# The first columns of w_in in f32 on SyncE's queue, and batch 1's kv products by halves

## Chip, cores, metric

The kernel runs on one core of a Trainium2 chip. The metric is the device time of one execution in microseconds (us). Engine names are those of the profile: PE is TensorE (PEld its weight loads), ACT ScalarE, DVE VectorE, POOL GpSimd, SP SyncE.

## What is computed

Two blocks follow each other: a linear attention and a feed-forward layer with a "snake" activation. Cut to what matters:

```python
# q, k, v: (8 batches, 8 heads, 576 tokens, 64)
q_s = softmax(q, axis=-1)          # over the 64 features of a token
k_s = softmax(k, axis=2)           # over the 576 tokens
kv  = einsum('bhsd,bhse->bhde', k_s, v)
att = einsum('bhsd,bhde->bhse', q_s, kv)

x = att.transpose(0, 2, 1, 3).reshape(4608, 512)    # tokens x model dim
h = x @ w_in                       # (512, 2048)
g = h + sin(alpha * h)**2 / alpha
out = g @ w_out                    # (2048, 512)
```

All inputs and the output are f32 in HBM; the kernel multiplies in bf16.

## The kernel before

**Tiling.** A batch has 576 tokens, held as 64 groups of J = 9 tokens (P = 64); with two head groups (e) that makes 128 partitions. `xT`, the transposed input of the feed-forward layer, lies in SBUF as 4 blocks of 128 model dims by 4608 tokens. The feed-forward layer goes over the tokens in nine tiles of MF = 512, which don't fall together with the batches: token tile 0 needs batch 0's first 8 of 9 groups, tile 1 needs the ninth and 7 of batch 1's, and so on. d_ff is cut in nN = 16 blocks of 128.

**Attention of a batch.** ScalarE takes exponentials of q and k (`exp_q`, `exp_k`, L117). `norm_q` (L139 to L146) sums and divides on VectorE, or on VectorE and GpSimd; TensorE (L186) or a DMA (L196) transposes the result into `qT`. v is cast into `vb` with a column of ones (`cast_v`, L131). `kv_mm` (L157) multiplies keys by values: for a model-dim half ii, 9 x 2 products of 64 rows by 130 columns. `kv_norm` (L167, L170) divides by the column of sums into `kbd`, a block-diagonal matrix, whose halves of the model dims are [:, e, ii]. `attn_out` (L206, evicted at L209) or `attn_chunk` (L214) multiplies `qT` by `kbd` into PSUM, which a copy casts into `xT`.

**Feed-forward of a token tile.** `mm_h` (L234) does four products of 512 columns for each of 16 blocks; `sine` takes the sine on ScalarE (L240) and the square on ScalarE (L242), GpSimd (L244) or VectorE (L246); `combine` on VectorE (L250) makes g. `mm_o` (L254) does 64 products of 512 columns for a tile, evicted at L260 and stored at L263. `take(os, n)` puts the next n of these output products into TensorE's order, so they can be laid between other work. The order of each engine's work is that of the program text (`manual_schedule`); each engine takes its instructions in order.

**The start.** SyncE's queue carries q, k and v of batch 0 (L94, L275). GpSimd waits for the first half of k (`held`, L313) and then issues the loads of w_in, which cast f32 to bf16 on their way (L107): columns 0 to 255, 256 to 511, and three times 512 columns, each as two DMAs, one for each half x of the model dims; then the first two of four parts of w_out (L110). The view of w_in is

```python
win_v = moe_w_in.rearrange("(x c d) n -> x d c n", x=2, c=4)
```

so the row of w_in is x * 256 + c * 64 + d: partition 64 x + d holds it in block c. TensorE does warm-up products (L302), batch 0's transposes, kv and output products, and begins token tile 0 with the products of blocks 0 and 1 (columns 0 to 255 of w_in). Loads of batch 1's q and k are issued within token tile 0, after blocks 6 and 13 (`late`). The loads use a pool of 5 staging tiles (`stage`), taken in turn.

**Batch 1** lies in token tile 0's output products: 10 of them, the ninth group of batch 0 (L214, copied at L390), 36 more, the transposes, 12 more, both halves of kv, one norm over both, 3 more, and then for each half two `attn_out` of 4 and 5 groups and one output product. Two PSUM buffers (`ps_e`) serve the kv and output products. Then token tile 1 begins. Its output products (`o_stream(1)`) carry batch 2's attention in the same way.

Of the kernel before, what the change touches and what calls it, by code (L numbers as in the profile page):

```python
# [15 lines left out]
F32 = mybir.dt.float32  # L16
# [7 lines left out]
def kernel(  # L24
# [14 lines left out]
    nc = tc.nc  # L39
    ctx.enter_context(nc.allow_non_contiguous_dma(reason="layout"))  # L40
    B, H, S, D = q.shape
# [3 lines left out]
    J = 9  # L45
    P = S // J
# [8 lines left out]
    stage = ctx.enter_context(tc.tile_pool(name="stage", bufs=5))  # L55
# [11 lines left out]
    xT = singles.tile([128, 4, NT], BF16, name="xT")  # L67
    win = singles.tile([128, 4, d_ff], BF16, name="win")
# [7 lines left out]
    def src_view(t, b):  # L76
        return t[b].rearrange("(i e) (p j) d -> (e p) i (j d)", e=2, j=J)

    win_v = moe_w_in.rearrange("(x c d) n -> x d c n", x=2, c=4)
# [5 lines left out]
    def load(name, t, b, halves=False, eng=nc.sync, gate=None):  # L85

        st = stage.tile([128, 4, J, D], F32, name=f"st_{name}", tag="st")
        for ii in range(2) if gate else ():
            gate(st[:, ii, 0, 0:1], zero)
        view = src_view(t, b)  # L90
        flat = st.rearrange("p i j d -> p i (j d)")
        if halves:
            for ii in range(2):
                eng.dma_start(out=flat[:, ii::2], in_=view[:, ii::2])  # L94
        else:
            eng.dma_start(out=flat, in_=view)
        staged[name, b] = st
# [6 lines left out]
    def load_win(c0, c1):  # L104
        n = slice(c0, c1)
        for x in range(2):
            nc.gpsimd.dma_start(out=win[64 * x:64 * x + 64, :, n], in_=win_v[x][:, :, n])  # L107

    def load_wout(c):
        nc.gpsimd.dma_start(out=wout[:, 4 * c:4 * c + 4, :], in_=wout_v[:, 4 * c:4 * c + 4, :])  # L110
# [38 lines left out]
    def kv_mm(b, ii, pool, split=False):  # L149

        if ii == 0 or split:
            A["kvp", b] = pool.tile([128, 2, 512], F32, name="kvp", tag="a")
        kvp, ke, vt = A["kvp", b], A["ke", b], vb[b % 2]
        for j in range(J):
            for e in range(2):
                r = slice(64 * e, 64 * e + 64)
                nc.tensor.matmul(kvp[:, e, ii * 130:(ii + 1) * 130],  # L157
                                 ke[r, j, ii * 128:(ii + 1) * 128],
                                 vt[r, j, ii * 130:(ii + 1) * 130],
                                 start=(j == 0), stop=(j == J - 1))  # L160

    def kv_norm(b, i0=0, i1=2):

        kt, m = kbd[b % 2], i1 - i0
        kvr = small.tile([128, 2, 2, 2], F32, name="kvr")[:, :, 0:m]
        src = A["kvp", b][:, :, i0 * 130:i1 * 130].rearrange("p e (ii x c) -> p e ii x c", ii=m, x=2)
        nc.vector.reciprocal(kvr, src[:, :, :, :, D])  # L167
        for x in range(2):
            r = slice(64 * x, 64 * x + 64)
            nc.vector.tensor_tensor(kt[r, :, i0:i1, r], src[r, :, :, x, 0:D],  # L170
                                    kvr[r, :, :, x].unsqueeze(3).to_broadcast([64, 2, m, D]), op=ALU.mult)
# [28 lines left out]
    def attn_out(b, ii, half, pool, eng):  # L200
        qT, kt = A["qT", b], kbd[b % 2]
        j0, j1 = XO[half]
        n = (j1 - j0) * P
        xp = pool.tile([128, 2, 512], F32, name="xp", tag="a")
        for e in range(2):
            nc.tensor.matmul(xp[:, e, 0:n], kt[:, e, ii], qT[:, ii, j0:j1, e * 64:(e + 1) * 64],  # L206
                             start=True, stop=True)
        c0 = (J * b + j0) * P
        eng(xT[:, 2 * ii:2 * ii + 2, c0:c0 + n], xp[:, :, 0:n])  # L209

    def attn_chunk(b, c, j0, j1, xp):

        ii, e = divmod(c, 2)
        nc.tensor.matmul(xp, kbd[b % 2][:, e, ii], A["qT", b][:, ii, j0:j1, e * 64:(e + 1) * 64],  # L214
                         start=True, stop=True)
# [6 lines left out]
    def mm_h(t, ni, wide=None, k0=0, k1=4):  # L222

        if ni == 0 and k0 == 0:
            G[t] = gpool.tile([128, nN, MF], BF16, name="g")
        if k0:
            hp = HP[t, ni]
        elif wide and ni % 6 in ((2, 3) if t == 0 else (4, 5)):
            hp = wide()
        else:  # L230
            hp = ps_h.tile([128, MF], F32, name="hp", tag="h")
        HP[t, ni] = hp
        for ki in range(k0, k1):
            nc.tensor.matmul(hp, win[:, ki, ni * 128:(ni + 1) * 128],  # L234
                             xT[:, ki, t * MF:(t + 1) * MF], start=(ki == 0), stop=(ki == 3))
        return hp
# [30 lines left out]
    ACT_CP, DVE_CP, GP_CP = nc.scalar.copy, nc.vector.tensor_copy, nc.gpsimd.tensor_copy  # L267
# [6 lines left out]
    for ii, j0, j1 in VJ:  # L274
        nc.sync.dma_start(out=st[:, ii::2, j0:j1].rearrange("p i j d -> p i (j d)"),  # L275
                          in_=src_view(v, 0)[:, ii::2, j0 * D:j1 * D])
    make_identity(nc, ident)
    DVE_CP(identb, ident)
    zero = singles.tile([128, 1], F32, name="zero")
# [7 lines left out]
    ps_e = ES.enter_context(tc.tile_pool(name="ps_e", bufs=2, space=PSUM, reuse_waits="tile"))  # L287
# [23 lines left out]
    q_tile(0)  # L311

    GP_CP(singles.tile([128, 1], F32, name="held"), staged["k", 0][:, 0, 0, 0:1])  # L313
    for c0, c1 in ((0, 256), (256, 512), (512, 1024), (1024, 1536), (1536, 2048)):
        load_win(c0, c1)
    for c in range(2):
        load_wout(c)
    q_transpose_ii(0, 0, 0, 8, tps[0])
# [14 lines left out]
    for c in range(4):  # L333
        xp = ps_h.tile([128, MF], F32, name="hp", tag="h")
# [4 lines left out]
    def h_slot(t, ni, sq, lag, wide=None):  # L339
        hp = mm_h(t, ni, wide, 2 if t < 2 and ni < 2 else 0)  # L340
        lag.append((t, ni, hp, sine(t, ni, hp, sq)))

    def flush(lag, keep):
        while len(lag) > keep:
            combine(*lag.pop(0))
# [14 lines left out]
    def take(it, n=1000):  # L360
        for _ in range(n):
            if next(it, 0) == 0:
                return
# [4 lines left out]
    with ES:  # L368
        def lent():
            return ps_e.tile([128, 2, MF], F32, name="hh", tag="a")[:, 0]  # L370

        late = {6: lambda: load("q", q, 1, halves=True, gate=DVE_CP), 8: lambda: load_wout(2),
                10: lambda: load_wout(3), 13: lambda: load("k", k, 1, halves=True, gate=DVE_CP)}
        for ki in range(2):
            for ni in range(2):
                mm_h(0, ni, lent, ki, ki + 1)
        for ni in range(nN):
            h_slot(0, ni, "DPAPPAPPAPPAPPAP"[ni], lag, lent)
            flush(lag, 1)
            if ni in late:  # L380
                late[ni]()
        flush(lag, 0)

        accs = [ps_h.tile([128, dm], F32, name="hp", tag="h") for _ in range(4)]
        os = o_quad(0, accs, [DVE_CP, ACT_CP, DVE_CP, ACT_CP])
        take(os, 10)
        xp = ps_e.tile([128, 4, P], F32, name="xp", tag="a")
        for c in range(4):
            attn_chunk(0, c, 8, 9, xp[:, c])
        ACT_CP(xT[:, :, 8 * P:9 * P], xp)  # L390
        take(os, 36)
        exp_q(1)
        load("v", v, 1, halves=True)
        load_batch(2)
        norm_q(1, [GP, V])
        exp_k(1)
        for ii in range(2):
            q_transpose(1, ii, ps_e, DVE_CP)
        cast_v(1, [ACT_CP, DVE_CP])
        nc.scalar.activation(zero, zero, AX.Sin)  # L400
        take(os, 12)
        kv_mm(1, 0, ps_e)
        kv_mm(1, 1, ps_e)
        kv_norm(1)
        take(os, 3)
        for ii in range(2):
            attn_out(1, ii, 0, ps_e, DVE_CP)
            attn_out(1, ii, 1, ps_e, ACT_CP)
            take(os, 1)
        take(os)  # L410
        load("q", q, 3)
        load("k", k, 3)

        for ki in range(2):
            for ni in range(2):
                mm_h(1, ni, lent, ki, ki + 1)
        for ni in range(nN):
            h_slot(1, ni, SQ[ni], lag, lent)
            flush(lag, 1)
        cast_v(2, [GP_CP, GP_CP])  # L420
        flush(lag, 0)

    ps_o = ctx.enter_context(tc.tile_pool(name="ps_o", bufs=2, space=PSUM, reuse_waits="tile"))
    ps_a = ctx.enter_context(tc.tile_pool(name="ps_a", bufs=1, space=PSUM, reuse_waits="tile"))
# [12 lines left out]
    exp_q(2)  # L437
    exp_k(2)
    os = o_stream(1)
    take(os, 16)  # L440
    norm_q(2, [GP, V])
    exp_q(3)
    exp_k(3)
# [11 lines left out]
    c0 = J * 2 * P  # L455
    for c in range(4):
        xp = ps_h.tile([128, MF], F32, name="hp", tag="h")[:, 0:6 * P]
# [3 lines left out]
    xp = ps_a.tile([128, 2, 512], F32, name="xp", tag="a")[:, :, 0:6 * P]  # L461
# [27 lines left out]
    for t in range(3, nT):  # L489
        b = t + 1 if t + 1 < B else None  # L490
        os = o_stream(t - 1)
# [56 lines left out]
```

The softmax here doesn't subtract the row's maximum and nothing guards it: scores larger than these inputs give would overflow.

## Time and profile before

| | |
|---|---|
| time, median of 3 runs | 291.37 us (291.19 to 291.61) |
| span of the profiled execution | 289.5 us |
| TensorE's first product of token tile 0 (L234) | starts at 15.38 us |
| TensorE's first product of token tile 1 (L234) | starts at 49.24 us |
| w_in's loads (L107) | issued from 8.82 to 15.3 us, 3.9 to 10.0 us from issue to landing |
| TensorE, ScalarE, VectorE, GpSimd busy | 95%, 79%, 65%, 28% of the span |

The page of the profile gives the busy time of each engine in the span, then a row for each engine over 40 equal slices of 7.24 us, in which a digit is the busy share in tenths. Busy time of TensorE is a model: a product of 512 columns is shown with 379 ns, but in a stream the next one starts 216 ns later, so what a stream takes is read from starts. A line of the timeline gives the start, the time that a run of equal instructions takes, engine and line, the operation with the tiles it writes and reads, how many there are, and in brackets how long the engine was idle before and what ended that. A line of the list of waits gives who waited for whom: the total, how often, the longest. A line of the DMA view gives for each queue its packets, MB and the time of its packets as a share of 16 DMA engines' time (over 100% when packets overlap); q1 is SyncE's queue, q0 GpSimd's.

### The profile page before, as it was taken

To read this page: it belongs to the slowest core of one execution; us is meant where nothing else is said; L and a number is where in the kernel's file an instruction comes from. 1 tells how busy PE (TensorE), PEld (TensorE's weight loads), DVE (VectorE), ACT (ScalarE), POOL (GpSimd) and SP (SyncE) were. 2 spreads that over 40 slices of the span, in tenths; PEclk is the share of its full clock that TensorE was granted. 3 is DMA by queue.
4 is the path that set the end of the run, shared out by engine and by line. 5 is a ranking of instruction groups with operands and counts; after the bars stand their busy time and mean duration, and the time that the engine had idled before them with its cause. 6 is when DMAs were issued, how large, how long until landed. Compare 5 with 4: busy or idle time off the path is not lost.

```text
span 289.5 us, 4230 instructions
## 1 busy us (share of the span) xinstructions
PE 274.8 (95%) x1543; PEld 131.2 (45%) x1570; DVE 187.7 (65%) x277; ACT 227.6 (79%) x322; POOL 80.4 (28%) x74
## 2 busy tenths in 40 slices
PE   2989998999999999999999999999999999999995
PEld 1434454444454445444444454445444444444443
DVE  3967586798958658774777567756775555545412
ACT  4789755999569899889987998799987777777500
POOL 0968420676685635002600070005000000000000
PEclk9999999999999999999999999999999999999999
DMA  7999999944899965109901893113311111111142
GB/s 263 306 174 232 275 371 408 310 189 135 201 161 389 399 198 127 33 20 344 314 14 33 298 307 77 37 39 84 70 39 36 36 36 39 36 37 36 39 110 72
DMA packets 37893, 45.77 MB, mean 158 GB/s; under 512 B 15968, under 2 KB 21360, under 8 KB 37872
## 3 DMA queue, kind: packets, MB, share of 16 engines
q1 hardware_dynamic: 32848, 41.16, 46.0%
q0 software_dynamic: 4832, 4.20, 9.4%
q8 instruction: 12, 0.20, 0.3%
q10 hardware_dynamic: 192, 0.14, 0.2%
q14 instruction: 9, 0.07, 0.1%
HBM read 36.71 MB, written 9.44 MB: 159 GB/s over the span
## 4 chain that ended last, share of the span: by engine, by line
PE 82%; DVE 6%; ACT 3%; POOL 3%; DMA 3%; issue 2%; ACTq 0%
PE hp L234 35%; PE op L254 34%; PE hp L254 4%; PE kvp L157 3%; POOL s L244 2%; PE xp L206 2%; DVE qs L144 2%; ACT s L240 1%; DMA st_q<-in_q_dram 1%; DMA qT<-qn 1%; PE op L234 1%; DVE g L250 1%; PE op L518 1%; PE hh L234 1%; DVE qn L146 1%
## 5 line engine op out<-in xcount | busy, mean ns | idle before, releaser
L250 DVE SCALAR_TENSOR_TENSOR g<-s,inva_sb,hp 128x512 bf16<-128x512 f32 x130 | 95.6, 746 | 63.9 <-ACT s L242 52.1
L234 PE MATMUL hp<-xT,win 128*128 128x512 bf16 x513 | 129.2, 379 | 1.2 <-DMA win<-in_moe_w_in_dram 0.6
L254 PE MATMUL op<-wout,g 128*128 128x512 bf16 x478 | 121.5, 379 | 1.4 <-issue 0.6
L240 ACT ACTIVATE s<-hp,alpha_sb 128x512 f32<-128x512 f32 x130 | 87.7, 682 | 26.5 <-PE hp L234 25.7
L234 PEld LDWEIGHTS <-win 128*128 128x128 bf16 x576 | 56.2, 98 | 68.9 <-issue 2.7
L254 PEld LDWEIGHTS <-g 128*128 128x128 bf16 x560 | 54.1, 98 | 61.8 <-issue 0.6
L242 ACT ACTIVATE s<-s 128x512 f32<-128x512 f32 x112 | 70.5, 630 | 3.6
L146 POOL TENSOR_TENSOR qn<-qe,qs 128x1152 bf16<-128x1152 bf16 x12 | 25.3, 2129 | 80.1 <-DVE qs L140 68.0
L244 POOL TENSOR_TENSOR s<-s 128x512 f32<-128x512 f32 x29 | 30.5, 1064 | 26.7 <-ACT s L240 26.2
L260 DVE COPY o<-op 128x512 f32<-128x512 f32 (+2 forms) x33 | 21.8, 662 | 9.9 <-PE op L254 6.0
L117 ACT ACTIVATE ke<-st_k 128x1152 bf16<-128x1152 f32 x16 | 17.8, 1151 | 4.2 <-DMA st_k<-in_k_dram 2.3
L139 DVE TENSOR_REDUCE qs<-qe 128x36 f32<-128x2304 bf16 x5 | 12.8, 2553 | 11.0 <-ACT qe L117 10.9
L117 ACT ACTIVATE qe<-st_q 128x1152 bf16<-128x1152 f32 x16 | 17.8, 1155 | 2.4 <-DMA st_q<-in_q_dram 2.4
L131 POOL CAST vb<-st_v 128x1152 bf16<-128x1152 f32 x12 | 13.6, 1165 | 5.9 <-DMA st_v<-in_v_dram 5.9
L209 DVE CAST xT<-xp 128x512 bf16<-128x512 f32 (+1 forms) x20 | 14.7, 736 | 0.7 <-PE xp L206 0.6
L254 PE MATMUL hp<-wout,g 128*128 128x512 bf16 x62 | 14.6, 379 | 0.2 <-issue 0.2
L144 DVE TENSOR_REDUCE qs<-qe 128x18 f32<-128x1152 bf16 x6 | 8.0, 1330 | 4.6 <-ACT qe L117 4.6
L206 PE MATMUL xp<-qT,kbd 128*128 128x256 bf16 (+1 forms) x48 | 9.5, 286 | 1.4 <-ACT xT L209 0.9
L117 ACT ACT_TABLE_LOAD x7 | 9.0, 1283 | 1.3 <-PEq L532 1.2
L157 PE MATMUL kvp<-vb,ke 64*128 64x130 bf16 x288 | 9.7, 216 | 0.0
L157 PEld LDWEIGHTS <-ke 64*128 64x128 bf16 x288 | 8.2, 93 | 3.2 <-issue 2.3
L234 PE MATMUL hh<-xT,win 128*128 128x512 bf16 x40 | 9.4, 379 | 0.0
(64 smaller groups left out, 115.3 us busy)
## 6 DMA issues: line engine op xcount, KB each, us to landing
out_dram<-o SPq DMA_DIRECT2D x70, 128.0 KB, 2.3
st_q<-in_q_dram SPq DMA_DIRECT2D x6, 1152.0 KB, 6.6
st_k<-in_k_dram SPq DMA_DIRECT2D x6, 1152.0 KB, 8.5
st_v<-in_v_dram SPq DMA_DIRECT2D x6, 1152.0 KB, 10.3
st_q<-in_q_dram SPq DMA_DIRECT2D x4, 576.0 KB, 5.8
st_k<-in_k_dram SPq DMA_DIRECT2D x4, 576.0 KB, 7.3
wout<-in_moe_w_out_dram POOLq DMA_DIRECT2D x4, 512.0 KB, 12.6
st_v<-in_v_dram SPq DMA_DIRECT2D x3, 576.0 KB, 10.7
```

What stands on the lines that cost most here:

```text
L117: nc.scalar.activation(dst[:, :, ii * 128:(ii + 1) * 128].rearrange("p j (x d) -> p x j d", x=2), src[:, ii::2], AX.Exp)
L146: engs[ii % len(engs)].tensor_tensor(qn[:, ii].rearrange("p j (x d) -> p j x d", x=2), qe[:, ii], part.unsqueeze(3).to_broadcast([128, J, ...
L157: nc.tensor.matmul(kvp[:, e, ii * 130:(ii + 1) * 130], ke[r, j, ii * 128:(ii + 1) * 128], vt[r, j, ii * 130:(ii + 1) * 130], start=(j == 0 ...
L206: nc.tensor.matmul(xp[:, e, 0:n], kt[:, e, ii], qT[:, ii, j0:j1, e * 64:(e + 1) * 64], start=True, stop=True)
L209: eng(xT[:, 2 * ii:2 * ii + 2, c0:c0 + n], xp[:, :, 0:n])
L234: nc.tensor.matmul(hp, win[:, ki, ni * 128:(ni + 1) * 128], xT[:, ki, t * MF:(t + 1) * MF], start=(ki == 0), stop=(ki == 3))
L240: nc.scalar.activation(s, hp, AX.Sin, scale=alpha_sb[:, ni:ni + 1])
L242: nc.scalar.activation(s, s, AX.Square)
L244: nc.gpsimd.tensor_tensor(s, s, s, op=ALU.mult)
L250: nc.vector.scalar_tensor_tensor(G[t][:, ni], in0=s, scalar=inva_sb[:, ni:ni + 1], in1=hp, op0=ALU.mult, op1=ALU.add)
L254: nc.tensor.matmul(acc, G[t][:, ni, j * 128:(j + 1) * 128], wout[:, ni, :], start=(ni == 0), stop=(ni == nN - 1))
L260: eng(o[:, cols], acc)
```

## The change

It has two parts. In the first, the first 256 columns of w_in no longer come by a casting DMA of GpSimd's queue: four DMAs on SyncE's queue, behind v, bring them in f32 into a staging tile, and GpSimd casts them (`GP_CP`) after it has issued the loads of columns 256 to 1535, and before those of columns 1536 up. It is meant to have the first columns there early, and to take their transfer out of GpSimd's queue. In the second, batch 1's kv products, norm and output products go by model-dim half, each half in a PSUM tile of its own, with output products of token tile 0 between them, so that TensorE has work while VectorE norms a half. Only the 7 groups that token tile 1 needs are made there; the other 2 come within the output products of token tile 1, in one copy.

```diff
         nc.sync.dma_start(out=st[:, ii::2, j0:j1].rearrange("p i j d -> p i (j d)"),
                           in_=src_view(v, 0)[:, ii::2, j0 * D:j1 * D])
+
+    wf = stage.tile([128, 4, J, D], F32, name="st_w", tag="st")[:, :, 0:4].rearrange("p c a b -> p c (a b)")
+    for c in range(4):
+        nc.sync.dma_start(out=wf[:, c], in_=win_v[:, :, c, 0:256])
...
     GP_CP(singles.tile([128, 1], F32, name="held"), staged["k", 0][:, 0, 0, 0:1])
-    for c0, c1 in ((0, 256), (256, 512), (512, 1024), (1024, 1536), (1536, 2048)):
+    for c0, c1 in ((256, 512), (512, 1024), (1024, 1536)):
         load_win(c0, c1)
+    GP_CP(win[:, :, 0:256], wf)
+    load_win(1536, 2048)
     for c in range(2):
         load_wout(c)
...
-        take(os, 12)
-        kv_mm(1, 0, ps_e)
-        kv_mm(1, 1, ps_e)
-        kv_norm(1)
-        take(os, 3)
+        take(os, 8)
+        kv_mm(1, 0, ps_e, split=True)
+        kv_norm(1, 0, 1)
+        take(os, 2)
+        kv_mm(1, 1, ps_e, split=True)
+        kv_norm(1, 1, 2)
+        take(os, 1)
+
+        c0 = J * P
         for ii in range(2):
-            attn_out(1, ii, 0, ps_e, DVE_CP)
-            attn_out(1, ii, 1, ps_e, ACT_CP)
-            take(os, 1)
+            xp = ps_e.tile([128, 2, 512], F32, name="xp", tag="a")[:, :, 0:7 * P]
+            for e in range(2):
+                attn_chunk(1, 2 * ii + e, 0, 7, xp[:, e])
+            (ACT_CP, DVE_CP)[ii](xT[:, 2 * ii:2 * ii + 2, c0:c0 + 7 * P], xp)
+            take(os, 2)
         take(os)
...
     os = o_stream(1)
-    take(os, 16)
+    take(os, 8)
+    xp = ps_a.tile([128, 4, 2 * P], F32, name="xp", tag="a")
+    for c in range(4):
+        attn_chunk(1, c, 7, 9, xp[:, c])
+    DVE_CP(xT[:, :, (J + 7) * P:2 * J * P], xp)
+    take(os, 8)
     norm_q(2, [GP, V])
```

## The prediction

> **What bounds the kernel now.** I read the engine shares and the row by slices first, then TensorE's waits, then the timelines of the two stretches that the change touches, then the DMA queues there.
>
> ```profile
> PE 274.8 (95%) x1543; PEld 131.2 (45%) x1570; DVE 187.7 (65%) x277; ACT 227.6 (79%) x322; POOL 80.4 (28%) x74
> ...
> PE   2989998999999999999999999999999999999995
> ...
> DMA  7999999944899965109901893113311111111142
> ```
>
> TensorE is full from the third slice to the last, so a change pays only where TensorE idles, and any new idle time is added to the end one for one. The DMA row is full over the first seven slices (50 us): this is where the change puts its transfers. The waits of TensorE (total, times, longest) are few:
>
> ```profile
> PE xp L206 <- ACT xT L209: 0.9, 2, 0.6
> ...
> PE hp L214 <- DVE kbd L170: 0.6, 2, 0.4
> PE hp L234 <- DMA win<-in_moe_w_in_dram: 0.6, 1, 0.6
> PE xp L206 <- DVE kbd L170: 0.4, 1, 0.4
> ```
>
> The third is w_in's: the timeline of TensorE at the start has
>
> ```profile
> 15.38 1.95 PE L234 MATMUL hp<-xT,win 128*128 128x512 bf16 x7
> 17.17 1.89 PE L234 MATMUL hh<-xT,win 128*128 128x512 bf16 x8
> 19.61 0.59 PE L234 MATMUL hp<-xT,win 128*128 128x512 bf16 x2 [0.55 <-DMA win<-in_moe_w_in_dram]
> ```
>
> so columns 0 to 511 are there in time at 15.38, and 0.55 us is lost on columns 512 up. The L206 waits are batch 1's, in this stretch:
>
> ```profile
> 44.28 1.40 PE L157 MATMUL kvp<-vb,ke 64*128 64x130 bf16 x36
> 45.84 0.59 PE L254 MATMUL hp<-wout,g 128*128 128x512 bf16 x2 [0.16 <-issue]
> 46.88 0.66 PE L206 MATMUL xp<-qT,kbd 128*128 128x256 bf16 x4 [0.44 <-DVE kbd L170]
> ...
> 48.32 0.65 PE L206 MATMUL xp<-qT,kbd 128*128 128x256 bf16 x4 [0.57 <-ACT xT L209]
> ```
>
> Last, the DMA queues (packets, MB, share of 16 engines), first in 5 to 9 us, where SyncE's queue is alone, then in 27 to 41 us, where it meets GpSimd's:
>
> ```profile
> q1 hardware_dynamic: 759, 1.64, 104.2%
> ```
> ```profile
> q1 hardware_dynamic: 1361, 2.97, 58.1%
> q0 software_dynamic: 1305, 1.29, 54.8%
> ```
>
> Alone it moves 1.64 MB in 4 us, 410 GB/s, so 25.6 GB/s for each of 16 engines. GpSimd's queue alone, in 16 to 24 us, writes 1.60 MB in bf16, 200 GB/s. Where both have work, each has about half of the engines' time.
>
> **What the Trainium skill says.** "DMA: Bandwidth & Descriptors", section "Why a DMA increments its semaphore by 16 and not by 1": a DMA need not use all 16 engines. The generator takes the slowest dimension (of a size other than 1) of source and of destination and uses the largest number up to 16 that divides both; for SyncE these are the lowest-numbered engines. Every load in the kernel before has 128, 64 or 16 there, so its trace shows only the case of 16 and can't confirm the rule. The same page, "Queues, rings and completion order": each engine goes round the queues that have work for it, packet by packet, and within one queue in order; the half shares of 27 to 41 us agree. "TensorE: Matmul & The Clock Gate", section "The HAM clock gate": after an idle window of some 3.4 us TensorE runs at half rate until it has been busy about as long. The trace agrees at its start: warm-up matmuls (L302) follow each other at 0.43 us from 5.81 to 10.15, and 512-column matmuls at 0.216 later (16 in 3.62 us with an end of 0.38).
>
> **The new w_in load.** The four DMAs read win_v[:, :, c, 0:256]: 2 halves (x) of 64 rows of 256 columns; x and d don't merge, since c lies between them. Source 2, destination 128: the rule gives **2 engines**, the same two for all four DMAs. The present loads avoid this, as each takes one x and has 64 on both sides.
>
> Landing. The DMAs stand behind v in SyncE's queue; v is read out at 11.7 (q1 moves its last 0.14 MB within 11 to 12). They carry 4 x 128 x 1 KB = 0.524 MB, 0.262 MB on each of two engines: at 25.6 GB/s, 10.2 us. From 11 us these engines also have their sixteenth of GpSimd's loads: columns 256 to 1535 are 1.31 MB in bf16, at 200 GB/s 6.5 us. Both queues must be served, and at half shares GpSimd's part is done first, so w lands at 11.7 + 10.2 + 6.5 = 28.4. If SyncE's queue were always served first: 11.7 + 10.2 = 21.9.
>
> The cast. GpSimd casts 128x1152 in 1.17 us (L131), so 128x1024 in 1.04; with 0.3 for hand-over, columns 0 to 255 are ready at 29.8. The first product of the first token tile needs them, and TensorE takes its work in order: it starts at 29.8 where it started at 15.38. **Cost 14.4 us**, nothing beside it, for TensorE has nothing else to do. Behind the cast, GpSimd holds the load of columns 1536 up (needed ten products' pace later, some 10 us; 0.26 MB halves land in about 4 us on a free queue), the first two w_out loads (needed after 14 us) and the squares of L244 (issue ends 2.9 us after the cast, first square needed at about 3.2): I cost these at nothing, hidden by ScalarE's 13.7 us of sines and squares in that tile.
>
> After 14 us idle TensorE is cold: some 9 of its first matmuls take 0.43 instead of 0.216, 1.9 us. Of this 0.5 is free, since ScalarE's first sine waited for its table load until 17.47 although its sixth matmul ended at about 16.9; in the changed kernel that load lies in the wait. Cost **1.4** (1.0 to 2.0). The 0.55 us wait on columns 512 up goes, but inside this same stretch, where ScalarE is then the later one: counted at nothing.
>
> **Batch 1 by halves.** From 41.60 to 49.24, 7.64 us, TensorE does 18 output products (18 x 0.216 = 3.9), 36 kv products (1.2, as in the row at 70.14) and 8 xp products of 2304 columns together (0.97): 6.05, so 1.6 is lost. Split, the norm of half 0 (0.18 + 2 x 0.28, as batch 0's at 13.24 = 0.75) lies beside 2 output products and 18 kv products (1.03); that of half 1 beside 3 output and 2 xp products (1.03); the last eviction (0.69) beside 5 output products (1.08). I leave 0.2 for hand-overs: **saves 1.4**. The first kv comes 4 output products earlier and needs v's cast; in before that would wait 0.5 (cast done at 43.92, TensorE there at 43.4), but after a late start the loads of batch 1 meet emptier queues. The last two columns of batch 1 move into the first output stream: 4 products of 128 columns (0.22) that are no longer in xp, and one eviction of 0.69 on VectorE ahead of norm_q(2), which is busy from 65.6 to 72.5; transposes of batch 2 may come up to 0.5 later. I take nothing and keep 0.5 for the range.
>
> The stage buffer: one tile more in a pool of 5 makes each later load of batches 1 and 2 follow an earlier tile; those are free before 16 us in the kernel before, so no wait. The four issues take SyncE 2 us after 4.5, and nothing stands behind them until batch 1's q at 24.
>
> Sum: 291.4 + 14.4 + 1.4 - 1.4 = **305.8**.
>
> **Rivals.** (1) Sixteen engines after all, if the instruction that reaches the generator has another outer dimension. Then w shares all engines with GpSimd's queue: 0.524 MB at 205 GB/s, 2.6 us, lands at 14.3, cast by 15.6, TensorE starts 0.2 later, loses no 0.55 and saves 1.4: 291.4 + 0.2 - 0.5 - 1.4 = 289.7, faster. For it: nothing in the trace has shown fewer than 16 engines. Against: the shape in the code. (2) Two engines, SyncE's packets served first: 21.9, cast by 23.3, cost 7.9: 299.3. For it: at 28 to 30 us q1 has 77% of the engines against 32%. Against: at 33 us it is 12% against 113%, and half over the whole. (3) Two engines that also fall back as in 14 to 16 us, where GpSimd's queue writes only 93 GB/s: 2 to 3 us more, and batch 1 saves nothing: 310.
>
> **Chances.** Two engines with shared time (the forecast and its slow form (3)) 0.64, two engines served first 0.18, sixteen engines 0.18 (of which 0.15 faster, 0.02 same, 0.01 slower). So faster 0.15, same 0.02, slower 0.83. The range takes in the first two with their bounds: rival (2) with 1.8 saved and 1.0 cold, 298.5, less a little, to 311; the sixteen engines are left out.
>
> **What would show it.** Right: TensorE idle from about 15 to 30 us, waiting on POOL's cast; the cast waiting on st_w; st_w landing over 15 us after issue; a low DMA share between GpSimd's loads and the cast; 0.43 us spacing after the gap; no wait of L206 on L170 or L209 above 0.2. Wrong: st_w landing by 15 us (rule not in force, rival 1), or at 22 (rival 2); a gap ended by anything but the cast.

## The result and the profile after

The changed kernel takes 307.64 us (median of 4 runs, 307.05 to 308.04) beside 291.49 us of the kernel before (291.19 to 292.09): the ratio is 1.055, with a 95% interval of 1.0524 to 1.0576. It is slower by 16.2 us; the forecast was 305.8.

The engine shares and the rows by slices of the profile after (a slice is now 7.63 us):

```profile
PE 276.5 (91%) x1542; PEld 131.6 (43%) x1570; DVE 188.4 (62%) x280; ACT 227.5 (75%) x321; POOL 80.3 (26%) x73
...
PE   2900899999999989999999999999999999999995
...
PEclk9965699999999999999999999999999999999999
DMA  7961899999095998511891199111511111111142
```

TensorE has the same work (276.5 against 274.8 us), and two empty slices that were nearly full before. In the same slices the DMA row falls to 6 and 1: TensorE waits while the 16 DMA engines together are less and less busy. The granted clock of TensorE falls to 6, 5 and 6 tenths in the third to fifth slices, in the gap and just after it. TensorE's waits (total, times, longest), the new one and what is left of those at L206:

```profile
PE hp L234 <- POOL win L320: 15.7, 1, 15.7
...
PE xp L206 <- ACT xT L209: 0.3, 1, 0.3
```

One wait of 15.7 us is new, on GpSimd's cast (line 320 of the changed kernel). The waits on w_in's DMA and of L206 on L170 are gone, and that of L206 on L209 is 0.3 instead of 0.9; what is left of it lies in a later batch (L206's first product is now at 105.9 us, since batch 1 no longer uses that line). The timelines of GpSimd, TensorE and SyncE's queue there:

```profile
30.16 1.04 POOL L320 CAST win<-st_w 128x1024 bf16<-128x1024 f32 x1 [17.35 <-DMA st_w<-in_moe_w_in_dram]
```
```profile
31.26 1.04 PE L234 MATMUL hp<-xT,win 128*128 128x512 bf16 x2 [15.74 <-POOL win L320]
32.51 2.34 PE L234 MATMUL hp<-xT,win 128*128 128x512 bf16 x5 [0.22 <-issue]
34.64 2.23 PE L234 MATMUL hh<-xT,win 128*128 128x512 bf16 x8
36.71 3.62 PE L234 MATMUL hp<-xT,win 128*128 128x512 bf16 x16
```
```profile
3.27 1.49 SPq L275 DMA_DIRECT2D st_v<-in_v_dram  x3
4.81 14.99 SPq L280 DMA_DIRECT2D st_w<-in_moe_w_in_dram  x4
```

The chain is read backwards: TensorE waits for the cast, the cast for st_w, and st_w lands at about 30.0 (an estimate from the start of the cast; the profile has no landing for it), although SyncE began to issue it at 4.81. The DMA queues in 20 to 25 us and in 26 to 29 us (packets, MB, share of 16 engines):

```profile
DMA packets 158, 0.15 MB, mean 31 GB/s; under 512 B 7, under 2 KB 158, under 8 KB 158
...
q0 software_dynamic: 77, 0.07, 8.7%
q1 hardware_dynamic: 81, 0.08, 5.8%
```
```profile
q1 hardware_dynamic: 144, 0.15, 13.6%
```

Alone, SyncE's queue uses 13.6% of sixteen engines, which is 2.2 of them, and moves 48 packets in a us, 24 for each of two engines: 24.6 GB/s for an engine. In 20 to 25 us each queue is down to 16 packets a us, one of GpSimd's for one of SyncE's, on a share of 2.3 engines together (14.5% of 16). So GpSimd's loads seem to have finished on the other fourteen.

The two profiled spans (305.3 and 289.5) differ by 15.8 us. By the starts of TensorE's work, they part into four stretches:

| stretch | before, us | after, us |
|---|---|---|
| to the first product of token tile 0 | 15.38 | 31.26 |
| from there to batch 0's ninth group (tile 0's products) | 17.28 | 18.50 |
| from there to token tile 1 (batch 1) | 16.58 | 15.01 |
| from there to the end | 240.26 | 240.53 |

### The profile page after: what moved, and what is told of

It reads as the page before. It is cut to its first block, busy times and chain, and to the rows that moved or that the text cites. A ratio compares the mean times of both kernels' runs of the same rounds, so it can differ in the third digit from the quotient of the medians.

```text
span 305.3 us, 4237 instructions
## 1 busy us (share of the span) xinstructions
PE 276.5 (91%) x1542; PEld 131.6 (43%) x1570; DVE 188.4 (62%) x280; ACT 227.5 (75%) x321; POOL 80.3 (26%) x73
## 3 DMA queue, kind: packets, MB, share of 16 engines
HBM read 36.71 MB, written 9.44 MB: 151 GB/s over the span
## 4 chain that ended last, share of the span: by engine, by line
PE 78%; DMA 7%; SPq 4%; POOL 3%; DVE 3%; issue 2%; ACT 2%; POOLq 0%; ACTq 0%
PE hp L234 34%; PE op L254 32%; DMA st_w<-in_moe_w_in_dram 6%; PE hp L254 4%; POOL s L244 2%; SPq L280 2%; PE kvp L157 2%; PE hh L234 1%; PE xp L206 1%; DMA qT<-qn 1%; DVE g L250 1%; PE op L535 1%; PE op L234 1%; ACT s L240 1%; DVE qs L144 1%
## 5 line engine op out<-in xcount | busy, mean ns | idle before, releaser
L234 PE MATMUL hp<-xT,win 128*128 128x512 bf16 x511 | 130.6, 382 | 16.8 <-POOL win L320 15.7
L234 PEld LDWEIGHTS <-win 128*128 128x128 bf16 x576 | 56.7, 99 | 85.5 <-POOL win L320 16.2
L131 POOL CAST vb<-st_v 128x1152 bf16<-128x1152 f32 x12 | 13.6, 1162 | 5.2 <-DMA st_v<-in_v_dram 5.2
L246 DVE TENSOR_TENSOR s<-s 128x512 f32<-128x512 f32 x3 | 2.5, 848 | 18.5 <-ACT s L240 18.5
L209 DVE CAST xT<-xp 128x512 bf16<-128x512 f32 (+1 forms) x18 | 13.4, 742 | 0.1
```

The lines of the kernel that those rows point to most:

```text
L131: engs[ii](vv[:, 2 * ii:2 * ii + 2, :, 0:D], staged["v", b][:, ii::2])
L234: nc.tensor.matmul(hp, win[:, ki, ni * 128:(ni + 1) * 128], xT[:, ki, t * MF:(t + 1) * MF], start=(ki == 0), stop=(ki == 3))
```

## The experiments

Theory A is the prediction's: the four DMAs run on 2 engines because of the outer dimension of their source, and that load is the whole loss. Theory B: SyncE's transfer is starved beside GpSimd's queue, whatever the number of engines. Theory C: the two parts of the change are not what they seem, the batch 1 part costs, or gains only because of the late start.

### The number of engines

**Outer dimension 4.** In this and the next two kernels only the rows that a DMA fetches differ, so they compute with other rows of w_in than the reference; four DMAs, bytes, queue and place are those of the changed kernel.

```diff
+    win_r = moe_w_in.rearrange("(a c d) n -> a c d n", a=4, c=4)
     for c in range(4):
-        nc.sync.dma_start(out=wf[:, c], in_=win_v[:, :, c, 0:256])
+        nc.sync.dma_start(out=wf[:, c], in_=win_r[:, c, :, 0:256])
```

> Four DMAs as in the changed kernel, but the 128 rows of each are taken as 4 groups of 32 instead of 2 of 64 (again other rows of w_in in the partitions, output not the reference's). Theory A: 4 engines with 128 packets each. In turn with GpSimd's 96 packets (32 small ones at 0.04 us, 64 at 0.075) that makes 128 x 0.041 + 6.1 = 11.3 us after 11.9: st_w lands at 23.2 (21.5 to 24.5); time about 301. If the number of engines is not set by this dimension: 30 us as in the changed kernel, or under 15.

**Outer dimension 8**: the same with a=8.

> The same with 8 groups of 16 rows (output not the reference's). Theory A: 8 engines with 64 packets each, in turn with GpSimd's first 64 (32 small, 32 large): 64 x 0.041 + 3.7 = 6.3 us after 11.9: st_w lands at 18.2 (17 to 19.5); time about 295.

**Outer dimension 128**: the same with `"(c p) n -> c p n"` and `win_r[c, :, 0:256]`.

> Four DMAs as in the changed kernel, but block c takes 128 rows of w_in that follow each other (so the partitions hold other rows of w_in than they should, and the output is not the reference's). Outer dimensions 128 and 128. Theory A: 16 engines, st_w lands by 15 us (16 if the last issue at 8 us leaves it behind GpSimd's first packets), time 289.5 to 292. A theory in which four DMAs in a row on SyncE are the trouble: 30 us, 307.

Measured, from the timelines of GpSimd and TensorE:

| outer dimension of the source | cast starts, us | token tile 0 starts, us | time, us |
|---|---|---|---|
| 2 (changed kernel) | 30.16 | 31.26 | 307.6 |
| 4 | 23.4 | 24.47 | 300.0 (one run) |
| 8 | 16.8 | 17.93 | 293.6 (one run) |
| 128 | 15.08 | 16.18 | 289.96, ratio 0.9934 (0.9915 to 0.9952) |

The row of the cast in GpSimd's timeline for 128, with 2.07 us of waiting for st_w where the changed kernel has 17.35:

```profile
15.08 1.04 POOL L321 CAST win<-st_w 128x1024 bf16<-128x1024 f32 x1 [2.07 <-DMA st_w<-in_moe_w_in_dram]
```

One number in the access pattern moves the start of the cast by 15 us. The rule of the Trainium skill ("DMA: Bandwidth & Descriptors", section "Why a DMA increments its semaphore by 16 and not by 1"), that the engines are the largest number up to 16 that divides both outer dimensions, ordered all four cases, and the arithmetic made from it gave 23.2 for 4 (the cast starts at 23.4) and 18.2 for 8 (16.8, so the forecast is at least 1.4 too late and the landing just under the stated 17). The packets agree: in 20 to 22 us each of the two queues moves 31 or 32 packets a us with 4, where it moves 16 with 2, so the pace of one engine is the same, 8 of each a us, and there are twice as many. That four DMAs follow each other on SyncE, or that they share with GpSimd, does not make the loss by itself: with 128 all that stays and the loss is gone. Theory B falls as the main cause.

**Halves, eight DMAs.**

```diff
     for c in range(4):
-        nc.sync.dma_start(out=wf[:, c], in_=win_v[:, :, c, 0:256])
+        for x in range(2):
+            nc.sync.dma_start(out=wf[64 * x:64 * x + 64, c], in_=win_v[x][:, c, 0:256])
```

> The f32 load of the changed kernel, but each of its four DMAs cut in two, one for each half x, so that both sides have 64 rows outermost; same bytes, same queue, same place. Theory A (the DMA runs on as many engines as divide both outer dimensions: 2 in the changed kernel, 16 here): st_w lands by 15.5 us, TensorE starts token tile 0 within 1.5 us of 15.4, time 289.5 to 291.5. Theory B (SyncE's queue is starved beside GpSimd's, whatever the number of engines): st_w lands near 30 us again and the time stays near 307.

Measured: 295.79 us, ratio 1.0129 (1.0093 to 1.0166). Neither theory's number: the cast started at 18.91 and token tile 0 at 20.00, and after a wait of 4.46 us tile 0's products were slow at first, as in the changed kernel (its stretch is 18.70). The list of waits of SyncE's queue in the first 20 us says why the load was late:

```profile
SPq L281 <- DMA st_k<-in_k_dram: 2.3, 2, 1.4
SPq L281 <- DMA st_v<-in_v_dram: 2.0, 3, 0.9
```

Each wait is for the DMA that SyncE had issued eight before, which fits a program that keeps eight completion counts and uses them in turn. So the last three of the eight waited until parts of v had landed, and the last was issued at 12.7. By then GpSimd's queue had most of the engines' time (132.9% in the us from 13, against 7.2% for SyncE's), and the DMA took 6.0 us to land. This is what there is of theory B's effect: in this run, a sixteen-engine transfer of 64 KB issued behind GpSimd's packets takes 6 us.

**Halves, two DMAs.**

```diff
-    for c in range(4):
-        nc.sync.dma_start(out=wf[:, c], in_=win_v[:, :, c, 0:256])
+    for x in range(2):
+        nc.sync.dma_start(out=wf[64 * x:64 * x + 64], in_=win_v[x][:, :, 0:256])
```

> The changed kernel with the f32 load as two DMAs, one for each half x (64 rows by 4 blocks by 256 columns), as GpSimd's loads are cut. Same bytes and place; both are issued by 5.5 us, while in the run with eight DMAs the last three were issued only when parts of v had landed, the last at 12.7. Theory A (16 engines, and issue early enough): st_w lands by 14.5 us, the cast ends by 15.6, TensorE starts within 0.5 us of 15.4, and the time is 289.3 to 291.0. Theory B (SyncE's transfer waits behind GpSimd's queue even with 16 engines): st_w lands at 17 us or later and the time is 293 or more.

Measured: 290.68 us, ratio 0.9958 (0.9939 to 0.9977). The time is theory A's, the landing lies between: cast at 16.49, token tile 0 at 17.59. Here v's last part landed late too (9.9 us after issue, against 8.5 with 128 rows), and TensorE's kv products waited 0.9 us for its cast; why v is later here was not settled. The profiled execution took 291.79, 1.1 us over the median, so its late landing need not be the usual one.

### Sharing with GpSimd's queue

```diff
-    for c0, c1 in ((256, 512), (512, 1024), (1024, 1536)):
-        load_win(c0, c1)
+    load_win(256, 512)
     GP_CP(win[:, :, 0:256], wf)
-    load_win(1536, 2048)
+    for c0, c1 in ((512, 1024), (1024, 1536), (1536, 2048)):
+        load_win(c0, c1)
```

> The changed kernel with only columns 256 to 511 loaded by GpSimd ahead of the cast; the loads of columns 512 to 1535 come behind it. Theory A with packets of the two queues taken in turn on the two engines: GpSimd's part before the cast falls from 1.31 to 0.26 MB, so st_w lands at about 11.9 + 10.7 + 1.3 = 24 us instead of 30.0; token tile 0 starts at 25, then waits up to 3 us on columns 512 up; time 301 to 304. If the landing were set by something else than the engines' shared work (the issue on SyncE, say), it would stay at 28 to 30 us and the time at 307 to 310.

Measured: 304.38 us, ratio 1.0429 (1.0398 to 1.0459); the cast started at 24.75. The cast is 5.4 us earlier with four fifths of GpSimd's bytes out of the way, where 6.5 - 1.3 = 5.2 were expected of the landing: on the two engines the queues' work adds up. The time misses the stated 304 by 0.4: besides 0.34 us on columns 512 up, TensorE lost 1.4 us waiting on w_out's loads, which this order pushes back, and that had not been counted.

### The cold TensorE

```diff
         HP[t, ni] = hp
+        for _ in range(72 if (t, ni, k0) == (0, 0, 0) else 0):
+            nc.tensor.matmul(hp, identb, A["qe", 0][:, 0:4, 0:128], start=True, stop=True)
         for ki in range(k0, k1):
```

> The changed kernel with 72 more warm-up products on TensorE just ahead of token tile 0, some 15.5 us of work that ends about when the cast does; they go into the PSUM tile that the first product then overwrites. Theory A (a cold TensorE costs the first tile 1.2 to 1.4 us beside the late start): from the first product to batch 0's ninth group 17.0 to 17.4 us instead of 18.5, and 306.3 instead of 307.6. If the longer first tile came from the loads behind the cast instead, it stays at 18.5 us and the time at 307.6.

Measured: 306.93 us, ratio 1.0526 (1.0498 to 1.0553). Cold is a TensorE whose granted clock is at half: in the changed kernel it is 0.50 from 31 to 34 us, 0.78 from 34 to 37, and 1.00 after that. Here the warm-up left a gap of only 0.86 us before the cast was done. TensorE's timeline at the start of tile 0 of this kernel:

```profile
31.89 1.90 PE L236 MATMUL hp<-xT,win 128*128 128x512 bf16 x8 [0.86 <-POOL win L322]
33.62 1.89 PE L236 MATMUL hh<-xT,win 128*128 128x512 bf16 x8
35.35 3.62 PE L236 MATMUL hp<-xT,win 128*128 128x512 bf16 x16
```

The first sixteen products take 3.46 us, from start to start (31.89 to 35.35); in the changed kernel they take 5.45 (31.26 to 36.71; one of them has no record). From the first product to batch 0's ninth group it is now 16.52 us, below the stated 17.0: cold TensorE costs this tile 2.0 us (18.50 - 16.52), not the 1.2 that the table shows, for the changed kernel also saves 0.8 there. The same 16.5 stands in the kernels whose load on sixteen engines finds TensorE warm (two DMAs, 128 rows). The 2.0 is of one execution: in the changed kernel without its second part, below, the clock comes back sooner, the first sixteen products take 4.85 us and the stretch is 17.90, so cold costs 1.4 there. A wait of 2.09 us was enough to bring it (outer dimension 8, where the first sixteen products take 5.14 us and the stretch is 18.19), less than the 3.4 us that the prediction names; the waits of 0.5 and 1.0 us with 128 rows and with two DMAs were not. Not all of it reached the end in the profiled run: token tile 0 started 0.6 us later than in the changed kernel, and a product of batch 2 waited 1.1 us for its DMA transpose, against 0.2.

### The two parts apart

**Batch 1 by halves alone**: the kernel before, with the second part of the change and not the first.

> The kernel before with the second part alone (batch 1 by halves). Theory A: this part saves 1.0 to 1.8 us, so 289.7 to 290.5, and the stretch from batch 0's ninth group to token tile 1 falls from 16.6 to about 15.0 us. Theory C (the second part gains only because the late start let batch 1's loads run ahead): the first kv product waits 0.5 us for v's cast, the gain is 0.9 us or less, 290.6 or more.

Measured: 291.10 us, ratio 0.9977 (0.9961 to 0.9994). The time and the wait are theory C's. Batch 1's stretch falls from 16.58 only to 16.20, for TensorE comes to the first kv product before v's cast; its list of waits has

```profile
PE kvp L157 <- ACT vb L131: 0.6, 1, 0.6
```

and the second half of v is cast by VectorE at 44.11, after 1.75 us of waiting for the load.

**The load alone**: the changed kernel without its second part.

> The changed kernel without its second part. Theory A: the load alone costs the 15.9 us by which token tile 0 starts late plus 1.2 us for a cold TensorE: 291.5 + 17.1 = 308.6, from 308 to 309.5. Theory C (the second part costs too): below 307.6.

Measured: 308.06 us, ratio 1.0549 (1.052 to 1.0578); token tile 0 starts at 31.43 and batch 1's stretch is 16.38. The times alone barely part the two kernels (both are 5.5% over the kernel before); the stretch does, 16.38 against 15.01. So the batch 1 part does not cost; after the late start it saves 1.4 us in its stretch of the profiled executions. The medians part by 0.4 only (308.06 against 307.64), and the profiled spans by 1.0, since tile 0's cold products took 0.6 less in the run without it (17.90 against 18.50). What the part is worth here in a whole execution is thus less sure than the stretch.

**The load alone on sixteen engines** (two DMAs, no second part).

> The f32 load as two DMAs on 16 engines, without the batch 1 part. Theory A: token tile 0 starts 1 to 2 us later than in the kernel before (after the cast), its first tile is 0.8 us shorter (no wait on columns 512 up), batch 1's stretch stays near 16.2 us: 291.2 to 292.2, no gain. With e2's small gain and e7's this tells whether the parts add: if they do, e7's 290.7 is this run minus 0.4 to 0.7; if the batch 1 part pays only with the emptier queues, minus 1 or more.

(e2 is the run with batch 1 alone, e7 the one with two DMAs.) Measured: 291.74 us, ratio 1.0 (0.9987 to 1.0013): nothing won, nothing lost. Token tile 0 starts 1.8 us late (17.21) and is 0.8 shorter. The profiled stretches do not add: batch 1's falls by 0.38 with the second part alone, by 0.2 with the load alone, and by 1.3 with both (two DMAs: 15.26). The medians say it more weakly: the second part brings 0.7 alone (291.83 to 291.10) and 1.1 on top of this load (291.74 to 290.68). It needs v in time, and with the load TensorE comes later and v sooner: the first half of batch 1's v takes 10.7 us from issue to landing in the kernel before and 11.0 with batch 1 alone, but 10.0 here, 9.9 with two DMAs and 9.6 in the version below.

### A version that beats both

```diff
-    for c in range(4):
-        nc.sync.dma_start(out=wf[:, c], in_=win_v[:, :, c, 0:256])
+    for h in range(2):
+        for x in range(2):
+            nc.sync.dma_start(out=wf[64 * x:64 * x + 64, 2 * h:2 * h + 2], in_=win_v[x][:, 2 * h:2 * h + 2, 0:256])
...
-    GP_CP(win[:, :, 0:256], wf)
+    for h in range(2):
+        GP_CP(win[:, 2 * h:2 * h + 2, 0:256], wf[:, 2 * h:2 * h + 2])
```

> A version meant to be better: the f32 load on 16 engines as four DMAs (two model-dim blocks by one half x each), and the cast in two, blocks 0 and 1 first, so that TensorE's first four products need half of the load. Theory A: the first products start 0.5 to 1 us earlier than with one cast behind two DMAs, and the time is 289.2 to 290.4. If the landing of the whole load behind GpSimd's first packets still sets the start, it equals the run with two DMAs, 290.7.

Measured: 290.12 us, ratio 0.9939 (0.9909 to 0.9969), 0.6% under the kernel before. GpSimd's timeline:

```profile
14.57 0.61 POOL L322 CAST win<-st_w 128x512 bf16<-128x512 f32 x1 [1.72 <-DMA st_w<-in_moe_w_in_dram]
15.57 0.61 POOL L322 CAST win<-st_w 128x512 bf16<-128x512 f32 x1 [0.38 <-DMA st_w<-in_moe_w_in_dram]
```

The first cast is done by 15.2, and TensorE's products start at 16.41 without a wait on it: batch 0's last products of L214 (15.97) and their eviction now come last, after 0.84 us of waiting for v's cast. Batch 1's stretch is 15.02.

## Why the prediction was right, and where its sizes were off

- **Two engines, and the start of token tile 0 as the place of the loss**: right, shown by the series over the outer dimension and by the share of 2.2 engines. The signs named came too: the idle time of TensorE ended by the cast, slow products after it, and no wait above 0.2 in batch 1.
- **The landing, 28.4 forecast and about 30.0 measured**, was the term most off; it makes 1.5 of the 1.9 us by which 305.8 fell short of 307.64 (the cost of the late start was 15.9 against 14.4). v had landed by 11.9, where 11.7 was taken. The load's own part is 256 packets at 24 a us: 10.7 instead of 10.2. The rest is the time beside GpSimd's part, 7.4 instead of 6.5. GpSimd's packets were not slower than priced: in 20 to 25 us a pair of one packet of each queue took about 0.125 us on an engine (8 of each a us). With SyncE's at 0.042, as when alone, 0.083 is left for GpSimd's, and 200 GB/s is 0.082 for 1 KB. Of the 0.9, 0.3 lies between the last packets (33 in the us from 29, at 48 a us) and the landing; the other 0.6 was not traced.
- **The share between the queues**: the Trainium skill's turn by packets ("Queues, rings and completion order") agrees, 77 packets to 81 in 20 to 25 us. Rival 2, in which SyncE's queue goes first, is out: the load did not land at 21.9.
- **The cast** took 1.04 as forecast, with 0.2 of hand-over.
- **The cold TensorE**: 1.4 forecast and 1.2 found in the sum, near by luck, for two sizes were off and nearly cancel. The forecast took 1.9 for the cold products, called 0.5 of it free because ScalarE's first sine had waited for its table load, and counted the end of the wait on columns 512 up at nothing. The run with warm-up shows 2.0 and none of it free; and the end of that wait is worth 0.8 (16.5 in the warm kernels against 17.28), more than the 0.55 of the profile, whose idle time counts from the modelled end of a product.
- **Batch 1, 1.4 forecast, 1.57 found**: right for this kernel. The prediction said that in the kernel before the first kv product would wait 0.5 for v's cast and that the late start would hide it; alone, the part waits 0.6 and saves 0.4 in its stretch.
- **Nothing taken for the moved last groups on VectorE**: the rest of the kernel is 0.27 longer than before, but 0.33 longer (240.59) in the run without the second part, so nothing can be put down to them.
- **Hidden work behind the cast**: no wait of TensorE on columns 1536 up or w_out appears in the changed kernel. It did appear for w_out (1.4 us) in the run that puts more loads behind the cast. The four issues on SyncE, priced at 2 us, took 15.0; nothing stood behind them until batch 1's q at 41.6, so this cost nothing.
- **Rival 1, sixteen engines at 289.7**: its size was fair. Sixteen engines and an early issue give 290.0 to 290.7, with a landing up to two us later than the 14.3 put there; with eight DMAs, issued late, they give 295.8.

## What to carry to other kernels

Look at the outermost dimension of both sides of every DMA as the program writes it: a view such as "(x c d) -> x d c" that can't merge leaves 2 in front, and here the transfer then had 2 of 16 engines; fewer loads of GpSimd beside it won back only 3.3 of the 16 us. Cut it so that a dimension of 64 or 128 rows stands in front on both sides. (Only the source's was varied here, on SyncE's queue.) And ask of a stage reworked to wait less whether its inputs are there: the batch 1 part alone won 0.2%, and the load on sixteen engines alone nothing, but together they won 0.4%, and with the cast split 0.6%.

## What was not expected of the hardware

- SyncE's issue of a two-engine DMA is not short. The four took 0.72, 1.80, 4.45 and 7.88 us (14.99 together, the SyncE line above), where the loads of v took about 0.5 each. With 4 engines the longest of the four took 2.45, with 8 it was 1.16 and with 16 (128 rows) 0.85. What holds the issue was not tried; the last one ended at 19.80, some 10 us before the load's last packets.
- In the kernel before, GpSimd's queue, alone and with work queued, wrote only 0.19 MB in 14 to 16 us, about half of its pace in 16 to 24 us; with batch 1 by halves alone, 0.23 MB. With the first columns off that queue the dip is gone: 0.38 to 0.39 MB in the same stretch of the two runs whose q0 lines follow, the split cast and the load alone on sixteen engines. The cause of the dip was not tried, and whether its end is what brings batch 1's v sooner is not shown.

```profile
q0 software_dynamic: 523, 0.38, 126.3%
```
```profile
q0 software_dynamic: 515, 0.39, 126.0%
```
